# Whole turns of a cosine through an integer tile, and another queue order where layer 2 begins

## The chip, the cores and the metric

The kernel runs on one core of one Trainium2 chip. The metric is the device time of one execution in microseconds (us); lower is better. Before the change the median of three runs is 1700.83 us (1698.61 to 1701.08). Engines are named as in the profile: PE is TensorE's matmuls, PEld its weight loads, DVE is VectorE, ACT is ScalarE, POOL is GpSimd, and SP is the queue that issues the DMAs. All loads and stores of this kernel stand in that one queue.

## What is computed

Attention over 8 batches, 8 heads, 576 positions, with keys and values averaged in groups of 8; its output is 4608 tokens of 512 columns. Two layers follow, each of 512 by 2048 by 512:

```python
def _moe_ref(x, w_in, w_out):        # layer 1
    h = x @ w_in
    g = h * np.cos(h)
    return (g @ w_out).astype(np.float32)

def _moe2_ref(x, w_in, w_out):       # layer 2
    h = x @ w_in
    relu6 = np.clip(h + 3.0, 0.0, 6.0)
    g = h * relu6 / 6.0
    return (g @ w_out).astype(np.float32)
```

## The kernel before

Every number of the matmuls is split into a high part, written by ACT as fp32r, and a low part, the difference, made by DVE or POOL; a product is three matmuls: high by high, high by low, low by high.

**Layer 1** walks over 144 steps. A step is one block of 512 tokens by 128 columns of the hidden layer: `gemm1` makes `h` in PSUM with 12 matmuls, a chain turns `h` into `g` = h cos(h), and `gemm2` takes `g` two steps later with 12 more. The chain of a step is, in program order: ACT `t` = h/2π + 0.25 (L288); ACT `g` = t + MAGIC, which rounds t to whole turns (L293); DVE `g` = (g − MAGIC) − t (L294); ACT `g` = sin(−2π g) (L297); DVE `g` = h·g (L301); ACT `gh`, the high part (L304); DVE or POOL `gl`, the low part (L310). Attention is cut into pieces that are recorded between the steps by a table of due numbers (`GOFF`), so that attention and layer 1 share the engines until about 450 us. Later steps carry, in the same way, the conversion of layer 2's weights (`quads`), which leave for `s_d` in DRAM, and the first seven operands of layer 2 (`split_small`).

**Layer 2** works on pairs of token blocks, `PAIRS`: the first has 256 columns a block, the other four 512. For each pair it runs seven products for each of four groups g (Strassen's scheme, class `Quad`): product n of group g takes the weight tile `wt[0, g, n]` and the operand `ops[pb, n]`. Twelve matmuls make one product. Between them, `Quad.end` evacuates: L899 and L910 (ACT) copy banks after product 1, L912 (DVE) adds after product 2, L917 (DVE) after product 4, and the function `gate` runs for products 3 to 6: ACT L970 (relu into a tile of the ring `take_r`), DVE L971 (times the input), and a store to `g_d` (L974). Product 4 needs L912 done, since it goes on in the bank that L912 reads; product 6 needs L917 in the same way.

The operands of the next pair are made by `make_op` (body `operand`): for some n a sum of input quarters (L705, L707, L709, L714), then the high part on ACT (L711), then the low part (L712). Their inputs come by four loads from `y_d` (`load_raw`, L851). Weight tiles come by `load_w` (L839), 28 for a layer half.

The order on each engine is set by a scheduler that takes the recorded program and its own estimates of durations; each engine then executes in that order, and an instruction that waits holds up all behind it on its engine. `tc.issue_after(x)` records that what is issued inside the block on the engine of x stays behind x there; it adds no wait on another engine.

Of the kernel before, what the change touches and what calls it, by code (L numbers as in the profile page):

```python
# [8 lines left out]
F32 = mybir.dt.float32  # L9
F32R = mybir.dt.float32r  # L10
BF16 = mybir.dt.bfloat16
U32 = mybir.dt.uint32
AF = mybir.ActivationFunctionType
# [6 lines left out]
MAGIC = 12582912.0  # L20
# [9 lines left out]
def tile_kernel(ctx, tc, q, k, v, wi1, wo1, wi2, wo2, ident_d, mask_d, out):  # L30
# [119 lines left out]
    def fetch_quads(m, u):  # L150
        wi, wo = words[1]
        for half in range(2):
            st = stg.tile([P, 2 * HW], U32, tag="st", name="st", bufs=2)
            for part in range(2):
                o = part if half else 1 - part
                if m == 0:
                    g, c = divmod(u, 2)
                    col = (o * (NF // 2) + 2 * g) * P * 2
                    src = wi[(half * 2 + c) * P : (half * 2 + c + 1) * P, col : col + HW]
                else:  # L160
                    row = (half * (NF // 2) + u) * P
                    src = wo[row : row + P, o * HW : (o + 1) * HW]
                nc.sync.dma_start(out=st[:, part * HW : (part + 1) * HW], in_=src)
            staged["q", m, u, half] = st

    def quads(m, u):

        wa = stg.tile([P, 1024], U32, tag="a", name="wa", bufs=2)
        wb = stg.tile([P, 1024], F32, tag="wb", name="wb", bufs=1)
        halves = {}  # L170

        def bits(half):
            st = staged["q", m, u, half]
            a = wa[:, half * HW : (half + 1) * HW]
            e = halves[half] = stg.tile([P, HW], BF16, tag="e", name="e")
            nc.scalar.activation(out=e, in_=st.bitcast(BF16)[:, 3::4], func=AF.Square)
# [9 lines left out]
        def value(half):  # L186
            st = staged.pop(("q", m, u, half))
            a = wa[:, half * HW : (half + 1) * HW]
# [5 lines left out]
                out=f(a), in0=halves[half], scalar=2.0**-30, in1=f(a), op0=ALU.is_ge, op1=ALU.mult  # L194
            )

        a21, a11, a12, a22 = (f(wa)[:, n * 256 : (n + 1) * 256] for n in range(4))
        s1, s2, s3, s4 = (wb[:, n * 256 : (n + 1) * 256] for n in range(4))

        def sums(part):  # L200
# [7 lines left out]
        def split(part):  # L208
            n, k0 = ((3, 0), (4, 3))[part]
            w = f(wa)[:, 256:] if part == 0 else wb  # L210
            at = 4 * (u % 2) + 2 * part
            hi, lo = (big(CONV[at + x])[:, : n * 256] for x in range(2))
# [3 lines left out]
            for h, t in ((0, hi), (1, lo)):  # L216
                if m == 0:
                    g, c = divmod(u, 2)
                    dst = d[g * 7 + k0 : g * 7 + k0 + n, :, c, h, :]
                else:  # L220
                    q, c = divmod(u, 2)
                    dst = d[q + 4 * k0 : q + 4 * (k0 + n - 1) + 1 : 4, :, c, h, :]
                nc.sync.dma_start(
                    out=dst.rearrange("t p x -> p t x"),
                    in_=f(t).rearrange("p (t x) -> p t x", x=256),
                )

        def fetch():
            if (m, u) != (1, 7):
                fetch_quads(*divmod(8 * m + u + 1, 8))  # L230
# [4 lines left out]
            [lambda: bits(0)],  # L235
            [lambda: before(0)],
            [lambda: value(0)],
            [lambda: bits(1), lambda: before(1)],
            [lambda: value(1), fetch],
            [lambda: sums(0)],  # L240
            [lambda: sums(1)],
        ]

# [423 lines left out]
    def w_ahead(s, odd):  # L667
        nonlocal quad_at
        if not running:
            if converted == len(wjobs):  # L670
                if s < SA + LAG or s >= SB:
                    return
                if quad_at == 16 and not quad_ops:
# [7 lines left out]
                elif not quad_ops:  # L681
                    if quad_at == 0:
                        fetch_quads(0, 0)
                    quad_ops.extend(quads(*divmod(quad_at, 8)))
# [273 lines left out]
    for n in range(28):  # L958
        load_w(0, n)
    for pb, (t0, w) in enumerate(PAIRS):  # L960
# [111 lines left out]
```

## Time and profile before

| | |
|---|---|
| median of 3 runs | 1700.83 us |
| the profiled execution | 1703.01 us, of which the span is 1701.2 us |
| PE busy | 1622.8 us, 95% of the span |
| DVE, ACT, POOL busy | 1162.1, 952.1, 351.1 us |
| mean granted clock of TensorE | 0.987 of full speed |

The span has four stages: attention alone (to about 75 us), attention with layer 1 (to about 450 us), layer 1 with the conversion of layer 2's weights (to 996 us) and layer 2. The windows view gives, for a stretch, the busy time of each engine and the share of the clock that TensorE was granted; the timeline gives single instructions with the idle time of their engine before them; the lines view groups instructions by line. A PE that is busy in the view all the time has no hole there, and the number of its matmuls tells its pace.

### The profile page before, as it was taken

What the parts mean: (1) busy time and instruction counts of PE and PEld (TensorE: products, weight loads), DVE (VectorE), ACT (ScalarE), POOL (GpSimd) and SP (SyncE); (2) the same over time, 40 slices, a digit from 0 to 9 for tenths busy, and PEclk for the clock granted to TensorE, in tenths of its full rate; (3) what the DMA queues carried; (4) which work ended last, traced back from release to release, by engine and by line L of the source; (5) the groups of instructions that cost most, each with busy time, mean ns of one, the idle gap of its engine ahead of it and who ended that gap; (6) DMA issues with size and microseconds to landing.
All of it is one profiled execution on the core that took longest, in us unless ns stands there. A gap on an engine that the chain in (4) does not pass through costs nothing. (4 is left out here: it accounts for less than half of the span.)

```text
span 1701.2 us, 21102 instructions
## 1 busy us (share of the span) xinstructions
PE 1622.8 (95%) x7658; PEld 1349.7 (79%) x7658; DVE 1162.1 (68%) x1579; ACT 952.1 (56%) x1393; POOL 351.1 (21%) x266
## 2 busy tenths in 40 slices
PE   4588899999999999999999999999999999999999
PEld 3466677888888888888888788888888888888889
DVE  7899866665777788887886444454454576768665
ACT  2477778788666666665665533344444344444444
POOL 3656544232323201111113002020201000000000
PEclk9799999999999999999999998999999999999999
DMA  7555533322433377665665373242438955344231
GB/s 230 180 162 184 184 103 127 118 85 90 144 113 112 108 236 236 198 209 175 198 204 164 126 281 137 116 169 100 149 123 326 332 212 183 116 143 140 84 112 38
DMA packets 154758, 274.07 MB, mean 161 GB/s; under 512 B 15776, under 2 KB 79392, under 8 KB 153632
## 3 DMA queue, kind: packets, MB, share of 16 engines
q1 hardware_dynamic: 154656, 272.74, 48.1%
q8 instruction: 60, 0.98, 0.2%
q14 instruction: 42, 0.34, 0.1%
HBM read 167.84 MB, written 104.86 MB: 160 GB/s over the span
## 5 line engine op out<-in xcount | busy, mean ns | idle before, releaser
L859 PE MATMUL bank<-wa,wb 128*128 128x512 f32 (+1 forms) x1368 | 291.9, 361 | 6.7 <-issue 5.7
L859 PEld LDWEIGHTS bank<-wa,wb 128*128 128x128 f32 x1368 | 234.4, 192 | 45.2 <-issue 6.1
L281 PE MATMUL h<-xh,wb 128*128 128x512 f32 x648 | 211.4, 389 | 0.1
L324 PE MATMUL y<-gh,wb 128*128 128x512 f32 x648 | 210.8, 389 | 0.0
L711 ACT ACTIVATE wa<-wu 128x1024 fp32r<-128x1024 f32 (+1 forms) x130 | 127.3, 980 | 142.9 <-PE bank L859 124.9
L859 PE MATMUL bank<-wu,wb 128*128 128x512 f32 (+1 forms) x792 | 198.4, 386 | 0.0
L281 PE MATMUL h<-xh,wa 128*128 128x512 f32 x504 | 174.8, 405 | 2.8 <-DVE g L301 1.2
L294 DVE SCALAR_TENSOR_TENSOR g<-g,t 128x512 f32<-128x512 f32 x144 | 112.4, 781 | 95.0 <-ACT g L293 94.4
L859 PEld LDWEIGHTS bank<-wu,wb 128*128 128x128 f32 x792 | 148.7, 188 | 29.9
L324 PE MATMUL y<-gh,wa 128*128 128x512 f32 x504 | 171.1, 398 | 0.0
L259 POOL TENSOR_TENSOR xl<-xr,xh 128x512 fp32r<-128x512 f32 x72 | 105.5, 1481 | 315.2 <-ACT xh L258 308.2
L281 PEld LDWEIGHTS h<-xh,wb 128*128 128x128 f32 x648 | 121.6, 188 | 25.6 <-ACT xh L258 0.6
L324 PEld LDWEIGHTS y<-gh,wb 128*128 128x128 f32 x648 | 121.7, 188 | 25.3
L297 ACT ACTIVATE g<-g 128x512 f32<-128x512 f32 x144 | 90.9, 631 | 78.4 <-DVE g L294 77.9
L304 ACT ACTIVATE gh<-g 128x512 fp32r<-128x512 f32 x144 | 90.2, 627 | 71.0 <-DVE g L301 70.8
L712 DVE TENSOR_TENSOR wa<-wu,wa 128x1024 fp32r<-128x1024 f32 (+1 forms) x80 | 89.5, 1123 | 55.9 <-ACT wa L711 55.8
L281 PE MATMUL h<-xl,wb 128*128 128x512 f32 x324 | 126.3, 390 | 1.1 <-POOL xl L259 1.1
L324 PE MATMUL y<-gl,wb 128*128 128x512 f32 x324 | 126.0, 389 | 0.0
L301 DVE TENSOR_TENSOR g<-h,g 128x512 f32<-128x512 f32 x144 | 98.6, 685 | 30.9 <-ACT g L297 30.7
L859 PE MATMUL bank<-wa,wa 128*128 128x512 f32 (+1 forms) x552 | 117.5, 359 | 0.0
L970 ACT ACTIVATE wu<-bank,bias_c 128x1024 f32<-128x1024 f32 (+1 forms) x60 | 61.8, 1030 | 98.3 <-PE bank L859 85.3
L281 PEld LDWEIGHTS h<-xh,wa 128*128 128x128 f32 x504 | 95.3, 190 | 23.5 <-issue 2.0
(157 smaller groups left out, 3021.8 us busy)
## 6 DMA issues: line engine op xcount, KB each, us to landing
g_d<-wu SPq DMA_DIRECT2D x64, 512.0 KB
wu<-g_d SPq DMA_DIRECT2D x56, 512.0 KB
xr<-x_d SPq DMA_DIRECT2D x72, 256.0 KB
wb<-s_d SPq DMA_DIRECT2D x36, 512.0 KB
s_d<-wa SPq DMA_DIRECT2D x32, 512.0 KB
s_d<-wa SPq DMA_DIRECT2D x32, 384.0 KB
raw<-in_k_dram SPq DMA_DIRECT2D x8, 1152.0 KB
yp_d<-ys SPq DMA_DIRECT2D x36, 256.0 KB
```

Source lines behind the costliest of these rows:

```text
L259: nc.gpsimd.tensor_tensor(out=xl, in0=t, in1=f(xh), op=ALU.subtract)
L281: nc.tensor.matmul(h, a[:, cs], z, start=(n == 0), stop=(n == 3 * NC - 1))
L294: mark[s] = nc.vector.scalar_tensor_tensor(out=g, in0=g, scalar=MAGIC, in1=t, op0=ALU.subtract, op1=ALU.subtract)
L297: nc.scalar.activation(out=g, in_=g, func=AF.Sin, scale=-TWO_PI)
L301: nc.vector.tensor_tensor(out=g, in0=hs[s], in1=g, op=ALU.mult)
L304: nc.scalar.activation(out=gh, in_=g, func=AF.Copy)
L324: nc.tensor.matmul(y[c], a, z, start=(first and n == 0), stop=(last and n == 2))
L711: nc.scalar.activation(out=hi, in_=src, func=AF.Copy)
L712: el.tensor_tensor(out=lo, in0=src, in1=f(hi), op=ALU.subtract)
L859: nc.tensor.matmul(bank[:, e, :wide], w[:, j, h, e], z[:, j], start=start and j == 0 and x == 0, stop=stop and j == 1 and x == 2, skip_gro ...
L970: nc.scalar.activation(out=r, in_=c, func=AF.Relu, bias=bias_c[:, 2:3], scale=1.0)
```

## The change

In the chain, `t` becomes an int32 tile, so that the write of L288 rounds h/2π + 0.25 to a whole number of turns. The instruction with MAGIC (L293) goes. DVE's instruction now reads `h` from PSUM and the integer tile, h/2π − t, and the sine takes π/2 as a bias tile. In `quads` code is regrouped into a class; its instructions are the same in kind, size and number.

At the start of layer 2, 21 of 28 weight loads are recorded first, then the four input loads of pair 1; the other seven weight loads stand behind the last store of group 0. The operands of pair 1 are made during groups 2 and 3 (table `EARLY`) and no longer during group 1; ACT's and DVE's part of each operand is kept behind the last gate of that moment. Two sums of pair 1 go from POOL to DVE. The ring for the gate's results has five tiles and not three in groups 0 to 2 of the first pair. Input loads of later pairs stand behind the last store of group 0.

```diff
     def chain0(s):
         g = gpl.tile([P, N], F32, tag="g", name="g", bufs=2)
-        t = gpl.tile([P, N], F32, tag="t", name="t", bufs=2)
+        t = gpl.tile([P, N], I32, tag="t", name="t", bufs=2)
         nc.scalar.activation(out=t, in_=hs[s], func=AF.Copy, bias=0.25, scale=INV_2PI)
         gs[s] = (g, t)
 
     def chain1(s):
         g, t = gs[s]
-        nc.scalar.activation(out=g, in_=t, func=AF.Copy, bias=MAGIC, scale=1.0)
         mark[s] = nc.vector.scalar_tensor_tensor(
-            out=g, in0=g, scalar=MAGIC, in1=t, op0=ALU.subtract, op1=ALU.subtract
+            out=g, in0=hs[s], scalar=INV_2PI, in1=t, op0=ALU.mult, op1=ALU.subtract
         )
-        nc.scalar.activation(out=g, in_=g, func=AF.Sin, scale=-TWO_PI)
+        nc.scalar.activation(out=g, in_=g, func=AF.Sin, scale=TWO_PI, bias=bias_c[:, 1:2])
...
     take_r = turn_of(["u16", "u17", "u18"])
+    take_r0 = turn_of(["u16", "u17", "u18", "u12", "u13"])
...
         hi, lo = (cols(big(tag), w) for tag in XO[n])
-        operand(n, raws, hi, lo, {1: pool, 2: vec, 4: vec, 3: pool}.get(n), pool if n > 3 else vec)
+        sums = vec if pb == 1 else pool
+        with tc.issue_after(last["a"].ins), tc.issue_after(last["v"].ins):
+            operand(n, raws, hi, lo, {1: sums, 2: vec, 4: vec, 3: sums}.get(n), pool if n > 3 else vec)
         ops[pb, n] = hi, lo
...
-    for n in range(28):
+    last = {}
+    EARLY = {(2, 0): 0, (2, 3): 1, (2, 5): 2, (2, 6): 3, (3, 0): 4, (3, 4): 5, (3, 6): 6}
+    for n in range(21):
         load_w(0, n)
+    raws = load_raw(1)
...
-            if more and g == (pb > 0):
-                raws = load_raw(pb + 1)
+            if more and pb > 0 and g == 1:
+                with tc.issue_after(last["s"].ins):
+                    raws = load_raw(pb + 1)
 
             def gate(i, t, c, pb=pb, g=g, w=w):
-                r = cols(take_r(), w)
+                r = cols((take_r if pb or g == 3 else take_r0)(), w)
...
-                if more and (pb == 0) * 2 + g == 3:
-                    make_op(pb + 1, n, raws)
+                x = EARLY.get((g, n)) if pb == 0 else n if g == 3 else None
+                if more and x is not None:
+                    make_op(pb + 1, x, raws)
...
+            if pb == g == 0:
+                with tc.issue_after(last["s"].ins):
+                    for n in range(21, 28):
+                        load_w(0, n)
```

The scheduler sets a new order on each engine. Three places follow, each as it stood and as it stands. The lines of the changed program are up to some 25 higher: L970 is now L993, L711 is L727, L712 is L728, L912 is L928, L917 is L933, L971 is L996, L839 is L855, L851 is L867.

**ACT, where layer 2 begins.** Before, from the bank copies of group 1 on:

```order
L899 ACTIVATE bank<-bank 128x2x256
L910 ACTIVATE wu_9291<-bank 128x512
L711 ACTIVATE wu_9272<-wu_9142 128x1024
L711 ACTIVATE wu_9293<-wu_9146 128x1024
L711 ACTIVATE wu_9332<-wu_9148 128x1024
L970 ACTIVATE wu_9255<-bank,bias_c 128x512
L711 ACTIVATE wu_9311<-wu_9142 128x1024
L970 ACTIVATE wu_9328<-bank,bias_c 128x512
L970 ACTIVATE wu_9351<-wu_9349,bias_c 128x512
```

Now, from the bank copies of group 1 to those of group 2:

```order
L915 ACTIVATE bank<-bank 128x2x256
L926 ACTIVATE wu_9143<-bank 128x512
L993 ACTIVATE wu_9170<-bank,bias_c 128x512
L993 ACTIVATE wu_9188<-wu_9186,bias_c 128x512
L993 ACTIVATE wu_9204<-bank,bias_c 128x512
L993 ACTIVATE wu_9220<-bank,bias_c 128x512
L727 ACTIVATE wu_9237<-wu_8984 128x1024
L915 ACTIVATE bank<-bank 128x2x256
```

Three high parts of pair 1 stood ahead of a gate of group 0 (the tile 9255) and of all gates of group 1; now no high part stands ahead of a gate of these two groups.

**DVE, groups 2 and 3 of the first pair.** Before, group 2 and the first sum of group 3:

```order
L912 TENSOR_TENSOR bank<-bank,wu_9428 128x2x256
L971 SCALAR_TENSOR_TENSOR wu_9455<-wu_9455,bank 128x512
L917 TENSOR_TENSOR wu_9471<-bank,wu_9428 128x512
L971 SCALAR_TENSOR_TENSOR wu_9473<-wu_9473,wu_9471 128x512
L971 SCALAR_TENSOR_TENSOR wu_9489<-wu_9489,bank 128x512
L971 SCALAR_TENSOR_TENSOR wu_9505<-wu_9505,bank 128x512
L912 TENSOR_TENSOR bank<-bank,wu_9537 128x2x256
```

Now, from the first gate of group 2 to the first sum of group 3:

```order
L996 SCALAR_TENSOR_TENSOR wu_9283<-wu_9283,bank 128x512
L721 TENSOR_TENSOR wu_8988<-wu_8986,wu_8988 128x1024
L933 TENSOR_TENSOR wu_9304<-bank,wu_9256 128x512
L728 TENSOR_TENSOR wu_9288<-wu_8988,wu_9287 128x1024
L996 SCALAR_TENSOR_TENSOR wu_9306<-wu_9306,wu_9304 128x512
L996 SCALAR_TENSOR_TENSOR wu_9322<-wu_9322,bank 128x512
L723 TENSOR_TENSOR wu_8984<-wu_8988,wu_8984 128x1024
L996 SCALAR_TENSOR_TENSOR wu_9343<-wu_9343,bank 128x512
L728 TENSOR_TENSOR wu_9348<-wu_8990,wu_9347 128x1024
L728 TENSOR_TENSOR wu_9327<-wu_8984,wu_9326 128x1024
L730 TENSOR_TENSOR wu_8990<-wu_8990,wu_8984 128x1024
L928 TENSOR_TENSOR bank<-bank,wu_9385 128x2x256
```

Operand work that stood in group 1 now stands here: one sum (L721) ahead of group 2's L933, and three 1024-wide operations ahead of group 3's L928.

**PE, attention beside layer 1.** The stretch behind the scores (L452, now L468) of a unit of attention. Before:

```order
L504 MATMUL ap_ps<-ident,e_106 128x128 x4
L281 MATMUL h<-xh,wa_417 128x512
L281 MATMUL h<-xh,wa_416 128x512
L281 MATMUL h<-xl,wa_416 128x512
L281 MATMUL h<-xh,wa_417 128x512
L281 MATMUL h<-xh,wa_416 128x512
L526 MATMUL ap_ps<-ident,e_109 128x128
L526 MATMUL ap_ps<-ident,e_106 128x128
L281 MATMUL h<-xl,wa_416 128x512
L452 MATMUL ap_ps<-kbd_104,qT 128x144 x2
```

Now:

```order
L298 MATMUL h<-xh,wa_417 128x512
L298 MATMUL h<-xh,wa_416 128x512
L298 MATMUL h<-xl,wa_416 128x512
L298 MATMUL h<-xh,wa_417 128x512
L298 MATMUL h<-xh,wa_416 128x512
L520 MATMUL ap_ps<-ident,e_106 128x128 x4
L542 MATMUL ap_ps<-ident,e_109 128x128
L542 MATMUL ap_ps<-ident,e_106 128x128
L298 MATMUL h<-xl,wa_416 128x512
L298 MATMUL h<-xh,wa_417 128x512
L340 MATMUL y_848<-gh,wa_205 128x512
L340 MATMUL y_848<-gl,wa_205 128x512
```

The transposes of unit 106 moved behind five matmuls of layer 1, and the next unit's scores, which stood right behind, follow only after a step's twelve products of `gemm2` and two more matmuls.

## Rows read from the trace of the kernel before

**Rows 1.** The page: busy time by engine, and the chain that ended last.

```profile
PE 1622.8 (95%) x7658; PEld 1349.7 (79%) x7658; DVE 1162.1 (68%) x1579; ACT 952.1 (56%) x1393; POOL 351.1 (21%) x266
PE 39%; ACT 0%; issue 0%
```

**Rows 2.** Windows: stretch and length, busy time and instructions by engine, granted clock, DMA.

```profile
core 0: us, PE busy (x) PEld busy (x) DVE busy (x) ACT busy (x) POOL busy (x), PEclk, DMA share, GB/s
75.00:100.00 25.00, 19.97 (x100) 14.22 (x99) 23.64 (x40) 16.35 (x29) 17.00 (x13) 0.98 0.37 109
100.00:150.00 50.00, 41.82 (x207) 32.26 (x206) 48.41 (x76) 37.39 (x61) 32.19 (x25) 0.97 0.62 193
150.00:200.00 50.00, 41.67 (x202) 33.09 (x201) 46.12 (x66) 37.98 (x67) 31.26 (x26) 0.97 0.59 191
200.00:250.00 50.00, 46.87 (x233) 38.09 (x234) 32.24 (x60) 35.85 (x60) 21.77 (x21) 0.97 0.37 112
250.00:300.00 50.00, 47.18 (x249) 39.30 (x248) 34.45 (x61) 40.99 (x67) 23.56 (x22) 1.00 0.40 129
300.00:450.00 150.00, 149.11 (x764) 124.39 (x763) 96.11 (x179) 117.98 (x197) 41.34 (x36) 1.00 0.32 104
450.00:900.00 450.00, 450.00 (x1987) 372.63 (x1986) 359.83 (x546) 285.24 (x473) 81.87 (x55) 1.00 0.56 178
900.00:950.00 50.00, 48.73 (x213) 39.48 (x212) 31.54 (x43) 28.76 (x48) 18.89 (x13) 1.00 0.37 111
1000.00:1050.00 50.00, 43.34 (x316) 41.85 (x316) 24.22 (x29) 20.39 (x28) 14.89 (x6) 0.90 0.60 212
1021.40:1031.60 10.20, 7.64 (x35) 7.08 (x34) 6.11 (x7) 3.32 (x5) 3.07 (x2) 0.50 0.38 125
1050.00:1650.00 600.00, 600.00 (x2649) 496.81 (x2648) 357.15 (x303) 265.21 (x253) 34.37 (x14) 1.00 0.46 164
```

**Rows 3.** Timeline from 1006 us, layer 2's beginning: start, length, instruction, idle before.

```profile
1006.20 6.04 PE L859 MATMUL bank<-wa,wb 128*128 128x256 f32 x49
...
1013.66 2.41 POOL L705 TENSOR_TENSOR wu<-wu,wu 128x1024 f32<-128x1024 f32 x1 [72.82 <-DMA wu<-y_d]
1016.09 2.00 ACT L711 ACTIVATE wu<-wu 128x1024 fp32r<-128x1024 f32 x2 [3.98 <-POOL wu L705]
...
1018.00 0.67 ACT L970 ACTIVATE wu<-bank,bias_c 128x512 f32<-128x512 f32 x1
...
1020.11 3.08 DVE L712 TENSOR_TENSOR wu<-wu,wu 128x1024 fp32r<-128x1024 f32 x1
...
1020.29 1.99 PE L859 MATMUL bank<-wa,wb 128*128 128x256 f32 x12 [4.10 <-issue]
...
1023.89 2.90 PE L859 MATMUL bank<-wa,wb 128*128 128x256 f32 x12 [1.61 <-issue]
...
1027.73 12.04 PE L859 MATMUL bank<-wa,wb 128*128 128x256 f32 x84 [0.95 <-ACT bank L899]
```

**Rows 4.** Lines by form, 996 to 1050 us: count, busy us, mean ns, idle before.

```profile
L912 DVE TENSOR_TENSOR bank<-bank,wu 128x512 f32<-128x512 f32 x4 | 2.8, 700 | 14.2 <-PE bank L859 14.2
L971 DVE SCALAR_TENSOR_TENSOR wu<-wu,bank 128x512 f32<-128x512 f32 x11 | 7.5, 684 | 6.7 <-ACT wu L970 6.7
L970 ACT ACTIVATE wu<-wu,bias_c 128x512 f32<-128x512 f32 x4 | 2.9, 722 | 4.5 <-DVE wu L917 4.5
L709 DVE TENSOR_TENSOR wu<-wu,wu 128x1024 f32<-128x1024 f32 x1 | 1.2, 1212 | 0.0
```

**Rows 5.** Lines, 150 to 300 us: the chain's instructions beside attention.

```profile
L294 DVE SCALAR_TENSOR_TENSOR g<-g,t 128x512 f32<-128x512 f32 x17 | 16.4, 968 | 6.3 <-ACT g L293 6.2
L301 DVE TENSOR_TENSOR g<-h,g 128x512 f32<-128x512 f32 x18 | 12.3, 682 | 5.6 <-ACT g L297 5.4
L297 ACT ACTIVATE g<-g 128x512 f32<-128x512 f32 x18 | 11.4, 631 | 10.5 <-DVE g L294 10.4
L293 ACT ACTIVATE g<-t 128x512 f32<-128x512 f32 x17 | 10.7, 629 | 0.4
```

**Rows 6.** Lines, whole span: an operation of mixed types, and one on strided integers.

```profile
L193 DVE SCALAR_TENSOR_TENSOR wa<-e,wa 128x512 f32<-128x512 bf16 x32 | 23.0, 719 | 0.2
L131 DVE SCALAR_TENSOR_TENSOR a<-st,a 128x512 uint32<-128x512 uint32 x32 | 28.8, 901 | 0.7
```

More of the change, by code (lines that the diff above doesn't have):

```diff
@@ L147, in convert_weights @@
         return [first, second, third]
[L150 to L176, printed above, removed]
+    class Unit:
+        def __init__(self, m, u, x=256, o=0):
+            self.m, self.u, self.x, self.o = m, u, x, o
+        def fetch(self, tile):
+            m, u, x = self.m, self.u, self.x
+            wi, wo = words[1]
+            self.st = []
+            for half in range(2):
+                st = tile(half)
+                for part in range(2):
+                    o = part if half else 1 - part
+                    if m == 0:
+                        g, c = divmod(u, 2)
+                        row, col = (half * 2 + c) * P, (o * (NF // 2) + 2 * g) * P * 2
+                    else:
+                        row, col = (half * (NF // 2) + u) * P, o * HW
+                    col += 2 * self.o
+                    src = (wi, wo)[m][row : row + P, col : col + 2 * x]
+                    nc.sync.dma_start(out=st[:, 2 * part * x : 2 * (part + 1) * x], in_=src)
+                self.st.append(st)
+        def begin(self, wa, wb, e):
+            self.wa, self.wb, self.e = wa, wb, e
+        def bits(self, half):
+            st, n = self.st[half], 2 * self.x
+            a = self.wa[:, half * n : (half + 1) * n]
+            self.flag = self.e()[:, :n]
+            nc.scalar.activation(out=self.flag, in_=st.bitcast(BF16)[:, 3::4], func=AF.Square)
@@ L184, in bits, with value @@
             )
-        def value(half):
-            st = staged.pop(("q", m, u, half))
-            a = wa[:, half * HW : (half + 1) * HW]
+        def value(self, half):
+            st, n = self.st[half], 2 * self.x
+            a = self.wa[:, half * n : (half + 1) * n]
             nc.vector.scalar_tensor_tensor(
@@ L193, in value, with sums @@
             nc.vector.scalar_tensor_tensor(
-                out=f(a), in0=halves[half], scalar=2.0**-30, in1=f(a), op0=ALU.is_ge, op1=ALU.mult
+                out=f(a), in0=self.flag, scalar=2.0**-30, in1=f(a), op0=ALU.is_ge, op1=ALU.mult
             )
-        a21, a11, a12, a22 = (f(wa)[:, n * 256 : (n + 1) * 256] for n in range(4))
-        s1, s2, s3, s4 = (wb[:, n * 256 : (n + 1) * 256] for n in range(4))
-        def sums(part):
+        def sums(self, part):
+            x = self.x
+            a21, a11, a12, a22 = (f(self.wa)[:, n * x : (n + 1) * x] for n in range(4))
+            s1, s2, s3, s4 = (self.wb[:, n * x : (n + 1) * x] for n in range(4))
             if part == 0:
@@ L206, in sums, with split @@
                 nc.vector.tensor_tensor(out=s4, in0=a12, in1=s2, op=ALU.subtract)
-        def split(part):
+        def split(self, part, tile):
+            x, m = self.x, self.m
             n, k0 = ((3, 0), (4, 3))[part]
-            w = f(wa)[:, 256:] if part == 0 else wb
-            at = 4 * (u % 2) + 2 * part
-            hi, lo = (big(CONV[at + x])[:, : n * 256] for x in range(2))
+            w = f(self.wa)[:, x : 4 * x] if part == 0 else self.wb
+            hi, lo = (tile(part, h, n * x) for h in range(2))
             nc.scalar.activation(out=hi, in_=w, func=AF.Copy)
@@ L234, in quads, with fetch_quads @@
         return [
-            [lambda: bits(0)],
+            [lambda: unit.bits(0)],
             [lambda: before(0)],
[L237 to L241, printed above, removed]
-        ]
+            [lambda: unit.value(0)],
+            [lambda: unit.bits(1), lambda: before(1)],
+            [lambda: unit.value(1), fetch],
+            [lambda: unit.sums(0)],
+            [lambda: unit.sums(1)],
+        ]
+    def fetch_quads(n):
+        units[n].fetch(lambda half: stg.tile([P, 2 * HW], U32, tag="st", name="st", bufs=2))
     unsplit = []
@@ L672, in w_ahead @@
                     return
-                if quad_at == 16 and not quad_ops:
+                if quad_at == len(units) and not quad_ops:
                     if unsplit:
```

40 lines of the change are left out of this document (23 added, 17 removed).

## Prediction

> **What bounds the kernel now.** I read the page first: PE is busy for 95% of the span, and the chain that ended last is PE alone [rows 1]. So the question is only where PE has holes, and the windows answer it [rows 2]. From 450 to 900 us PE is busy all the time, 1987 matmuls in 450 us, 226.5 ns each, and from 1050 to 1650 us the same, 2649 in 600 us, again 226.5 ns. Nothing that the change does to ACT, DVE or a queue can shorten these stretches; it can only open holes in them. Three places have holes. (1) From 75 to 450 us PE idles 5.0 + 8.2 + 8.3 + 3.1 + 2.8 + 0.9 = 28.3 us. There DVE is the fullest engine at first (23.64 of 25, 48.41 and 46.12 of 50 us up to 200 us), then ACT (35.85 and 40.99 of 50 us up to 300 us). (2) From 900 to 950 us PE idles 1.3 us. (3) From 1000 to 1050 us, where layer 2 begins, it idles 6.7 us and the granted clock is 0.90.
>
> The timeline of that last place shows the cause [rows 3]. PE stops after the products of group 1 for 4.10 us, then for 1.61 and 0.95 us. ACT's gate instruction L970 at 1018.00 us, whose bank PE needs again, stood behind two high parts (L711) of pair 1's operands, which had waited 3.98 us for POOL's sum L705, which had waited for its load from `y_d`. The work that PE needed at once was queued behind work for 20 us later. The clock then stood at 0.50, the 1.2 GHz level, for 10.2 us [rows 2], behind the idle 4.10 us.
>
> **The change, part by part. Layer 2's beginning.** The hole costs 6.7 us of idle time, plus the slow clock: in 1021.4 to 1031.6 us PE did 35 matmuls in 7.64 us busy; at the pace ahead of the hole, 49 in 6.04 us or 0.123 us each [rows 3], they take 4.3 us. That is 3.3 us more, 10.0 in all. The new order on ACT has no high part ahead of a gate in groups 0 and 1, so that this wait can't arise there. The input loads of pair 1 now stand ahead of seven weight loads. Those seven are needed one by one from group 3 on, 31 us after layer 2 begins (three groups of 84 matmuls at 0.123 us), the last at about 40 us, and stand behind stores that leave after some 12 us; seven tiles of 0.52 MB are 3.7 MB, and at the 212 GB/s of that stretch [rows 2] they take 17 us. The last arrives some 11 us early, so I cost them at nothing; their cover is groups 1 and 2, and a rate under 130 GB/s would use it up. The two more ring tiles take away waits of the gate for its stores and cost nothing.
>
> What is late next is DVE, which has the operands to make in groups 2 and 3. In group 2 the sum L721 stands ahead of L933. After product 3 come the gate's ACT part (0.67 us [rows 3]), its DVE part (0.68), the sum (1.21) and L933 (0.70): 3.3 us with rows of the same widths [rows 4]. Products 4 and 5 last 2 x 12 x 0.123 = 2.9 us, so that product 6 waits about 0.4 us, or 0.6 with some 0.05 us at each hand-over. In group 3 three 1024-wide operations, 3.6 us, stand between the last gate of group 2 and L928, whose result product 4 needs. From the end of group 2's products, the last gate needs 0.7 + 0.7 us, behind a backlog of about 2 us from group 2; 2 + 1.4 + 3.6 + 0.7 = 7.7 us, against four products, 5.9 us, that PE has to do: 1.8 us of waiting. Together 2.4 us. Bounds: none, if the backlog is smaller, and 6.1 us, if both POOL and DVE stretch each other: DVE's L712 at 1020.11 us took 3.08 us in place of 1.2 beside POOL's work [rows 3], and two such stretches are 3.7 us. I take 2.4, since DVE's long operations ahead of L928 have no POOL work beside them in the new order. POOL's three low parts follow in group 3 and later. **Net: 10.0 - 2.4 = 7.6 us less.**
>
> **The chain.** Per step ACT loses L293, 0.629 us [rows 5]. The sine gets a bias tile: the sine before took 631 ns, a relu with a bias tile on the same width from SBUF 722 [rows 4], so that it may cost 0 to 0.09 us more; I take 0.09. ACT's write of integers isn't shown by any row; I take L288's time as it is. On DVE, L294 reads two SBUF tiles and took 968 ns on average from 150 to 300 us, while L301, which reads `h` from PSUM and one SBUF tile, took 682 [rows 5]. The new instruction has L301's operands, so I take 682; a mix of types (bf16 and fp32) takes 719, and the upper end is 901, an operation on strided integers [rows 6].
>
> From 450 us on all this lies beside a full PE and is worth nothing. From 150 to 300 us DVE saves 17 x 0.286 = 4.9 us, which I count in full since DVE sets the pace for a third of it and attention hands its delay on. ACT saves 17 x 0.54 = 9.2 us in the same stretch, but PE idles only 5.9 us in 200 to 300 us, where ACT is the fuller one, at 77%; a load that falls by 6.5 us in 76.8, some 8%, takes about 0.5 us of that. Against it stands the new order on PE: the next unit's scores follow 15 matmuls of layer 1 later at one place. PE is not the full engine there, but DVE, which is, may wait for its scores; at 226.5 ns the eight matmuls by which, counted in the two orders, attention's pieces of some three units lie later on average cost 1.8 us once. Further on the two orders keep step. Net 4.9 + 0.5 - 1.8 = 3.6 us less. Bounds: 10.8 less (4.9 and all 5.9 us of ACT's stretch), and 5 more, if the displaced pieces cost at three places and DVE gains nothing.
>
> On that contention the Trainium skill (SBUF — State Buffer, section Who interferes with whom) says that a VectorE instruction with two SBUF inputs shares a read port with GpSimd, and one of the two blocks until the other is done, while one with a single SBUF input doesn't. By that rule L294's longer times would go entirely, as in the sum, and POOL, which makes most low parts there, would gain too; by the rows alone POOL's gain isn't priced.
>
> **900 to 950 us.** PE idles 1.3 us there. A shorter chain on ACT may free it; I take half, 0.6 us, between 0 and 1.3.
>
> **Sum.** The span of 1701.2 us, with 1.8 us around it, is the profiled 1703.0 us; 7.6 + 3.6 + 0.6 = 11.8 us less give 1691.2 there. The profiled execution lies 2.2 us above the median of the runs, so 1700.8 - 11.8 = **1689.0 us** is the forecast.
>
> **The rivals.** (A) DVE becomes the bound at layer 2's beginning. The waits in groups 2 and 3 grow to 6.1 us by the stretch above, and the clock falls to 0.50 again for the 3.3 us: 9.4 of the 10.0 us are gone, and only 0.6 + 3.6 + 0.6 = 4.8 us remain, 1696 us. For it: L712 at 3.08 us. Against it: PE idled 1.3 us around 940 us and the clock stayed at 1.00 [rows 2].
>
> The same rule of the skill speaks for (A), since the two sums that go from POOL to DVE have two SBUF inputs each.
>
> (B) The chain is worth much more. In the attention stretch ACT is in the way of DVE oftener than its share tells: DVE idled 6.3 us before L294, 6.2 of them for L293, which is gone [rows 5]. With the full 10.8 us there, the time is 1700.8 - 7.6 - 10.8 - 0.6 = 1681.8 us. Against it: up to 200 us DVE hardly idles. (C) The integers don't do what they are for: ACT's write or DVE's read of them is slower, 901 ns on DVE. Then DVE gains 17 x 0.067 = 1.1 us, less than the 1.8 of the order: 1700.8 - 7.6 + 0.7 - 0.6 = 1693.3 us. (D) Slower than before: the new order on PE starves DVE beside attention. Each time that scores stand 15 matmuls later, 3.4 us, and DVE has nothing else, attention slips by that much. To eat up the 8.2 us of the other two places and end 3.4 us above before takes 11.6 us, four such places without any gain on DVE; six places, with DVE's 4.9 us kept, give 1700.8 - 8.2 - 4.9 + 20.4 = 1708.1 us. For it: DVE is nearly full up to 200 us. Against it: one such place is seen, and after it the two orders run level.
>
> **How the numbers follow.** The forecast has 0.58, with its own range 1684 to 1694 us. (A) has 0.12, (B) 0.17, (C) 0.06, (D) 0.07. The range for 8 in 10 takes in the forecast's and (C)'s, most of (B) and half of (A): 1681 to 1697 us. A measurement of this kernel tells 0.2%, 3.4 us, from no change. Faster than 1697.4 us are the forecast, (B), (C) and less than half of (A): 0.86. Within 0.2% is the rest of (A): 0.07. Slower is (D): 0.07.
>
> **What would show it.** In the profile after, the stretch 1000 to 1050 us should show PE idle for 1 to 4 us and the clock at 1.00. DVE's instruction on `h` and `t` should take about 0.68 us throughout, never over 1 us; the sine 0.63 to 0.72 us. The full stretches must keep their 226.5 ns per matmul. Layer 2 should begin some 4 us sooner than at 996 us. The prediction is wrong if PE's idle time in 75 to 450 us grows, if group 3 waits for weights, or if new holes open in the stretches that were full.

## The result, and the profile after

The changed kernel takes 1680.61 us (median of 4 runs, 1678.92 to 1681.6) against 1699.72 us for the kernel before, timed beside it: a ratio of 0.9888, with a 95% interval of [0.9871, 0.9905]. The gain is 19.1 us; 11.8 were forecast, and 1680.6 lies just below the range that began at 1681. The profiled execution took 1681.6 us, with a span of 1679.8.

The page of the kernel after: busy time by engine, the granted clock by slice, and the chain that ended last.

```profile
PE 1615.1 (96%) x7658; PEld 1345.9 (80%) x7658; DVE 1140.6 (68%) x1581; ACT 883.7 (53%) x1249; POOL 331.0 (20%) x264
PEclk7799999999999999999999999999999999999999
PE 87%; DVE 5%; DMA 3%; ACT 2%; POOL 2%; issue 1%; SPq 0%; ACTq 0%; POOLq 0%; DVEq 0%
```

ACT is busy for 68 us less than in [rows 1], DVE for 21.5, and neither number is the gain. Windows of the kernel after, with the columns of [rows 2]:

```profile
75.00:100.00 25.00, 21.23 (x111) 15.56 (x110) 23.64 (x42) 16.60 (x27) 15.19 (x15) 1.00 0.42 124
100.00:150.00 50.00, 44.86 (x236) 35.56 (x235) 49.53 (x84) 41.10 (x69) 32.49 (x27) 1.00 0.67 209
150.00:200.00 50.00, 44.14 (x216) 36.06 (x215) 37.47 (x60) 34.82 (x60) 28.05 (x24) 0.93 0.56 181
250.00:300.00 50.00, 48.18 (x252) 40.21 (x251) 34.43 (x64) 37.52 (x58) 17.25 (x19) 1.00 0.34 109
450.00:900.00 450.00, 450.00 (x1987) 372.63 (x1986) 349.16 (x549) 243.76 (x387) 73.19 (x52) 1.00 0.58 181
900.00:950.00 50.00, 50.00 (x223) 41.39 (x222) 29.09 (x40) 23.61 (x38) 17.90 (x12) 1.00 0.33 104
1000.00:1050.00 50.00, 50.00 (x314) 45.14 (x314) 28.92 (x31) 24.67 (x31) 7.59 (x3) 1.00 0.44 166
```

Against [rows 2]: PE executes 111, 236 and 216 matmuls up to 200 us where it executed 100, 207 and 202. The full stretch still has 1987 in 450 us. From 900 to 950 us there are 223 in place of 213. From 1000 to 1050 us PE no longer idles, and the clock stays at 1.00.

Three marks in the two traces (the start of the last attention matmul, of layer 2's first matmul, and of its last) split the whole difference of the two spans, 21.4 us (the profile before lies above its median, so that this is 2.3 us more than the gain by the medians):

| stage, us | before | after | difference |
|---|---|---|---|
| to the last attention matmul | 425.1 | 414.9 | −10.2 |
| from there to layer 2 | 570.8 | 568.6 | −2.2 |
| layer 2 | 701.3 | 692.3 | −9.0 |
| behind its last matmul | 4.0 | 4.0 | 0 |

Half of the difference thus lies in attention, where 3.6 us were expected. The chain's instructions have the durations that were expected. Lines of the kernel after, 150 to 300 us (count, busy us, mean ns, idle before):

```profile
L313 ACT ACTIVATE g<-g,bias_c 128x512 f32<-128x512 f32 x18 | 13.0, 722 | 5.3 <-DVE g L310 5.1
L310 DVE SCALAR_TENSOR_TENSOR g<-h,t 128x512 f32<-128x512 f32 x18 | 12.3, 685 | 4.4 <-ACT t L305 4.4
L305 ACT ACTIVATE t<-h 128x512 int32<-128x512 f32 x18 | 10.7, 592 | 16.9 <-PE h L298 16.9
```

DVE's instruction fell from 968 ns (L294 in [rows 5]) to 685, the sine rose from 631 to 722, and the write of integers takes 592, as the float write L288 did in this stretch before. POOL's low part of the chain, which the sum had not priced, fell from 1485 to 1342 ns in this stretch; the last section tells what that goes with.

### The profile page after: what moved, and what is told of

Its sections match the earlier page's. It is cut to its first block, busy times and chain, and to the rows that moved or that the text cites. A ratio compares the mean times of both kernels' runs of the same rounds, so it can differ in the third digit from the quotient of the medians.

```text
span 1679.8 us, 21085 instructions
## 1 busy us (share of the span) xinstructions
PE 1615.1 (96%) x7658; PEld 1345.9 (80%) x7658; DVE 1140.6 (68%) x1581; ACT 883.7 (53%) x1249; POOL 331.0 (20%) x264
## 4 chain that ended last, share of the span: by engine, by line
PE 87%; DVE 5%; DMA 3%; ACT 2%; POOL 2%; issue 1%; SPq 0%; ACTq 0%; POOLq 0%; DVEq 0%
PE bank L875 41%; PE h L298 21%; PE y L340 21%; PE ap_ps L555 2%; PE ap_ps L468 1%; DMA raw<-in_v_dram 1%; DMA raw<-in_k_dram 1%; DMA xr<-x_d 1%; DVE raw L423 1%; DVE sm L490 1%; PE ap_ps L520 1%; POOL xl L276 1%; DVE ptl L525 0%; POOL e L494 0%; DVE e L479 0%
## 5 line engine op out<-in xcount | busy, mean ns | idle before, releaser
L875 PE MATMUL bank<-wa,wb 128*128 128x512 f32 (+1 forms) x1368 | 287.7, 358 | 0.0
L727 ACT ACTIVATE wa<-wu 128x1024 fp32r<-128x1024 f32 (+1 forms) x130 | 127.3, 980 | 142.6 <-PE bank L875 121.2
L310 DVE SCALAR_TENSOR_TENSOR g<-h,t 128x512 f32<-128x512 f32 x144 | 99.0, 688 | 104.6 <-ACT t L305 104.3
L276 POOL TENSOR_TENSOR xl<-xr,xh 128x512 fp32r<-128x512 f32 x72 | 100.0, 1401 | 324.6 <-ACT xh L275 319.5
L305 ACT ACTIVATE t<-h 128x512 int32<-128x512 f32 x144 | 85.5, 593 | 126.0 <-PE h L298 125.7
L313 ACT ACTIVATE g<-g,bias_c 128x512 f32<-128x512 f32 x144 | 104.2, 724 | 79.4 <-DVE g L310 78.9
L728 DVE TENSOR_TENSOR wa<-wu,wa 128x1024 fp32r<-128x1024 f32 (+1 forms) x80 | 89.5, 1123 | 56.9 <-ACT wa L727 56.8
```

Of the source, the lines that this page charges most:

```text
L276: nc.gpsimd.tensor_tensor(out=xl, in0=t, in1=f(xh), op=ALU.subtract)
L305: nc.scalar.activation(out=t, in_=hs[s], func=AF.Copy, bias=0.25, scale=INV_2PI)
L310: mark[s] = nc.vector.scalar_tensor_tensor(out=g, in0=hs[s], scalar=INV_2PI, in1=t, op0=ALU.mult, op1=ALU.subtract)
L313: nc.scalar.activation(out=g, in_=g, func=AF.Sin, scale=TWO_PI, bias=bias_c[:, 1:2])
L727: nc.scalar.activation(out=hi, in_=src, func=AF.Copy)
L728: el.tensor_tensor(out=lo, in0=src, in1=f(hi), op=ALU.subtract)
```

## The experiments

### The two halves apart

x1_cos is the kernel before with the chain's diff alone; x2_l2 is the changed kernel with the old chain.

> The kernel before with the cosine's change alone; layer 2 as before. If the two parts are independent, layer 1 ends as in the changed kernel, 12.4 us sooner than before (983.4 us and not 995.8 us on the profile), and the hole where layer 2 begins stays: about 1688 us. If the queue order of layer 2 had a share in the sooner end of layer 1, it ends later than 983 us.

> The changed kernel with the cosine as before (L293 and two SBUF operands on DVE). If the parts are independent, layer 1 ends at 996 us as before and only the hole of 9 us where layer 2 begins is gone: about 1691 us. The first PE wait of over 1 us behind 960 us should be missing.

Measured: x1_cos 1686.93 us, ratio 0.9929 [0.9915, 0.9944]; x2_l2 1691.37 us, ratio 0.9952 [0.9937, 0.9967]; the kernel before 1698.71 us there. The chain earns 11.8 us alone, layer 2's order 7.3, together 19.1. Each ratio's interval is some 5 us wide, so that the exact sum is luck; but the halves add up within that, layer 2's half is near the 7.6 us forecast for it, and the miss lies in the chain. In x1_cos attention ends at 412.2 us and layer 2's hole is still there; in x2_l2 attention ends at 422.7 us, and the hole is gone.

### The chain: which of its two savings

x3_sbuf lets DVE read two SBUF tiles again; x4_act gives ACT its extra step back. x3_sbuf changes what the cosine computes.

```
# x3_sbuf
-            out=g, in0=hs[s], scalar=INV_2PI, in1=t, op0=ALU.mult, op1=ALU.subtract
+            out=g, in0=t, scalar=INV_2PI, in1=t, op0=ALU.mult, op1=ALU.subtract
# x4_act
+        nc.scalar.activation(out=t, in_=t, func=AF.Copy, scale=1.0)
```

> The changed kernel, but DVE's instruction of the chain reads the integer tile twice and not h from PSUM: two SBUF operands as before, and still no extra ACT instruction (the argument of the cosine is wrong by that). Theory: DVE's time, stretched where two-SBUF instructions meet POOL, sets attention's pace; then attention ends late again, near 423 us (before 425, changed 415), and the time is about 1688 us. Rival, the ACT instruction that went is what counts: attention ends at 415 us and the time is 1681 us.

> The changed kernel with one more ACT instruction in the chain, a copy of the integer tile in place (0.6 us, the load and the length of the chain as before); DVE reads h from PSUM. Theory: attention ends near 416 us and the time is about 1682 us, since DVE's time is as in the changed kernel. Rival, ACT's load or the chain's length counts: attention ends near 425 us and the time is about 1690 us.

Measured: x3_sbuf 1687.17 us, ratio 0.9926 [0.9911, 0.9941]; x4_act 1683.9 us, ratio 0.9909 [0.9892, 0.9925]. From x2_l2's 1691.4 us, ACT's saving alone is then worth 4.2 us and DVE's alone 7.5. That reads like "DVE sets the pace", so the next pair took DVE's load away by another way: the addition of 1e-9 to the softmax sums, 40 instructions, is left out of the changed kernel (x5_no_eps) and of x2_l2 (x11_old_no_eps).

```
-        nc.vector.tensor_scalar(out=sm[:w], in0=sm[:w], scalar1=1e-9, scalar2=None, op0=ALU.add)
```

> The changed kernel without DVE's addition of 1e-9 to the sums of the softmax (L491, one instruction of 8 columns a unit, 40 in all; a sum of at least 1 in fp32 is left as it was by that addition). Theory, DVE's time is attention's time: the 12 of these instructions that lie between the attention matmuls 180 and 420 took 5.5 us there; that stretch shrinks by about 5 us, and by some 2 more before it, so that the time is about 1674 us. Rival, PE's order or ACT sets the pace there: within 2 us of the changed kernel's 1680.6.

> As the run before this one, but with the cosine as before (the old chain, the new order of layer 2, no addition of 1e-9). In that order the 12 additions took 9.5 us of DVE, 789 ns each, in the same stretch. Theory: attention's stretch shrinks by 7 to 9 us against the kernel with the new order of layer 2 alone, to about 1683 us in all. Rival: it stays at 1691 us.

Measured: x5_no_eps 1678.63 us, 0.9887 [0.9872, 0.9902]; x11_old_no_eps 1689.45 us, 0.9948 [0.9931, 0.9964]. From the 181st attention matmul to the last, DVE is busy for 12 and 14 us less than in the kernels that they come from. The medians are 2 us lower in both, the ratios by 0.0001 and 0.0004, well within their intervals. That DVE's busy time is passed on one to one, which would have brought 1674 and 1683 us, is refuted. But all four kernels have a weakness: the scheduler gave each an order of its own on every engine (in x3_sbuf some 200 of DVE's 1581 places differ from the changed kernel's), so that none shows an instruction's worth alone.

### Instructions and order apart

Kernels of this kind have two things that differ, the instructions and the order in which each engine issues them. The order can be held fixed. At the end of the program, each instruction is tied to the one that is to stand ahead of it on its engine, with an edge that sets the order and adds no wait:

```
+    for engine, deltas in orders.items():        # places as the other kernel has them
+        at, prev, mine = 0, None, real[engine]
...
+        for step in deltas:
+            at += step
+            if prev is not None:
+                tc.add_manual_dep(
+                    mine[at], prev.name,
+                    mybir.DependencyInfo(mybir.DependencyClass.NoSync, mybir.DependencyReason.DATA),
+                    reason="order",
+                )
+            prev = mine[at]
```

> The kernel with layer 2's change and the old cosine chain (1691.4 us; attention ends at 422.7 us), but every engine issues its instructions in the order that the changed kernel has; the 144 roundings on ScalarE stand one place behind the write of t. If the shorter instructions earn the chain's 10 us, nothing changes: 1691 us, attention's end at about 423 us. If the scheduler's new order earns them, the time falls to that of the changed kernel, 1681 us, attention's end at about 413 us, with DVE's instruction of the chain still near 900 ns and ScalarE as busy as before. Between the two, the share tells.

> The changed kernel, all its instructions as they are, but every engine issues them in the order of the kernel with layer 2's change and the old chain. If the instructions earn the 10 us: 1681 us, attention's end at about 413 us. If the new order earns them: 1691 us and 423 us, although DVE's instruction of the chain takes 680 ns and ScalarE has 144 instructions less. If both are needed, both pinned kernels stay near 1691 us; if either is enough, both come to 1681 us.

Measured: x12_old_chain_new_order 1707.27 us, ratio 1.0042 [1.0027, 1.0056], so slower than the kernel before; x13_new_chain_old_order 1684.17 us, 0.9907 [0.9887, 0.9927]. Neither expectation had it that the new order harms the old chain. Part of that is where the step stands that the new order has no place for, ACT's rounding: in x12_old_chain_new_order another ACT instruction comes between the write of `t` and the rounding in 56 of 144 steps. The four corners (old or new chain, old or new order) were then timed side by side, in x15_old_chain_new_order with the rounding always directly behind the write of `t`.

> The changed kernel once more, beside the three others: 1680.6 us by the first result; attention's end within 3 us of 414.9 us. New instructions, new order.

> The kernel with layer 2's change and the old chain once more: 1691.4 us by the first look. Old instructions, old order.

> New instructions, old order, once more. If the instructions alone earn all, it equals r_after (1680.6 us). By the first run they earn 7 of the 10.8 us: 1684 us. If the first run was a lucky one and the order is what counts, it comes near r_old_chain (1691 us).

> Old instructions, new order, with the rounding on ScalarE always directly behind the write of t. If the 1707 us of the run before came from where the rounding stood, this comes down to about 1688 us, order alone then being worth some 3 us. If the new order doesn't fit the old chain, it stays above 1700 us, with holes behind 450 us as before.

| median, us (ratio, 95% interval) | old order | new order |
|---|---|---|
| old chain | 1688.91 (0.9943 [0.9927, 0.996]) | 1695.82 (0.9978 [0.9968, 0.9987]) |
| new chain | 1685.54 (0.9918 [0.9902, 0.9935]) | 1678.86 (0.9876 [0.9854, 0.9897]) |

The instructions alone earn 3.4 us in the old order. The new order alone costs 6.9 us. Both together earn 10.1. In the new order the instructions are thus worth 17.0 us, five times as much as in the old one; by the intervals, about 13 to 21 us against 0 to 8. x15_old_chain_new_order came out between its two expectations: moving the rounding took back 11.5 of x12_old_chain_new_order's 1707.27 us, and the rest of the loss stayed. So the 17.0 us hold for this place of the rounding, and would be more for the other. The windows show more (columns as in [rows 2]). First r_after, new chain in the new order:

```profile
75.00:175.00 100.00, 86.29 (x442) 66.88 (x442) 95.69 (x162) 75.51 (x126) 64.46 (x57) 0.99 0.58 178
175.00:425.00 250.00, 245.40 (x1255) 203.88 (x1254) 161.22 (x303) 183.05 (x293) 87.28 (x83) 0.99 0.38 122
```

r_old_chain, old chain in the old order:

```profile
75.00:175.00 100.00, 82.45 (x392) 63.68 (x391) 95.41 (x146) 70.59 (x121) 60.51 (x49) 0.93 0.57 178
175.00:425.00 250.00, 242.09 (x1254) 199.85 (x1254) 168.70 (x307) 201.37 (x331) 100.32 (x89) 1.00 0.36 115
```

r_new_chain_old_order:

```profile
75.00:175.00 100.00, 84.55 (x409) 65.41 (x408) 95.33 (x151) 69.48 (x116) 57.58 (x49) 0.94 0.57 178
175.00:425.00 250.00, 243.90 (x1259) 200.87 (x1258) 162.23 (x309) 187.30 (x300) 94.62 (x90) 1.00 0.37 119
```

x15_old_chain_new_order:

```profile
75.00:175.00 100.00, 85.19 (x438) 65.51 (x436) 96.30 (x162) 79.56 (x134) 62.72 (x53) 1.00 0.57 176
175.00:425.00 250.00, 236.78 (x1212) 195.89 (x1213) 158.59 (x294) 193.78 (x318) 91.76 (x85) 0.99 0.36 115
```

In the first 100 us the order decides: 442 and 438 matmuls in the new one, 392 and 409 in the old one, nearly whatever the chain (all other profiles of the new order have 438 to 443, and those of the old one 397 to 407). The granted clock is 0.99 and 1.00 against 0.93 and 0.94; it is not the order's alone, since x16_sbuf_new_order below, in the new order too, has 0.96 there with 439 matmuls. In the next 250 us the new order needs the new chain: 1255 matmuls with it, 1212 without, while the old order does 1254 and 1259 with either. There the old chain in the new order gives back 42 of the 46 matmuls that it was ahead (of the old chain's two profiled executions, x15_old_chain_new_order's lies 2.7 us below its kernel's median and r_old_chain's 3.4 us above; they are 0.8 us apart where the medians are 6.9, so that the loss itself is shown by the times and not by these windows). The first profile of the changed kernel has 1243 matmuls there, so that 12 of the 43 between 1255 and 1212 can be scatter.

Two last kernels keep the new order and give back one of the two savings each: the changed kernel with DVE's two SBUF reads (x16_sbuf_new_order), and with ACT's extra step (x17_act_new_order). The edits are those of x3_sbuf and x4_act.

> The changed kernel, every engine in the changed kernel's order, but DVE's instruction of the chain reads the integer tile twice (two SBUF operands in place of h from PSUM and one of SBUF; this changes what the cosine computes). If the reads are what the new order can't bear: DVE's instruction near 0.9 us and 1690 us or more. If ScalarE's extra step is: 1679 to 1683 us, although DVE's instruction is as long.

> The changed kernel in the changed kernel's order, with one more ScalarE instruction per step that rewrites t in place, directly behind the write of t. If ScalarE's extra step is what the new order can't bear: 1690 us or more, with a stall near 940 us. If the reads are: 1679 to 1683 us. If the two add up, the two losses make 17 us together.

Measured: x16_sbuf_new_order 1683.93 us, 0.9906 [0.9891, 0.9922]; x17_act_new_order 1688.33 us, 0.9932 [0.992, 0.9945]; the kernel before 1699.25 us there. Against r_after's ratio of 0.9876, the reads cost 5.1 us and ACT's step 9.5, which makes 14.6 of the 17 us. r_after was timed on another occasion, and the intervals leave about 1 to 10 us for the reads and 5 to 14 for the step; between the two kernels, timed together, it is 4.4 us, 1 to 8. So both matter, and ACT's step more. That step is a whole one of 632 ns, where the change saves ACT 0.54 us a step net of the slower sine. The waits of PE, 175 to 425 us (line that waits, line waited for: us in total, times, longest), name the place (scores are L468 in r_after, L469 and L470 in the two others). r_after:

```profile
PE ap_ps L468 <- DVE ptl L525: 3.2, 3, 1.9
```

The changed kernel's first profile (after):

```profile
PE ap_ps L468 <- DVE ptl L525: 5.2, 4, 2.1
```

x17_act_new_order:

```profile
PE ap_ps L469 <- DVE ptl L526: 7.3, 7, 3.0
```

x15_old_chain_new_order:

```profile
PE ap_ps L470 <- DVE ptl L527: 9.6, 7, 3.8
```

PE's scores wait for a bank that DVE frees with `ptl`. What holds DVE up is seen in its lines, 150 to 300 us, in x17_act_new_order:

```profile
L311 DVE SCALAR_TENSOR_TENSOR g<-h,t 128x512 f32<-128x512 f32 x18 | 12.4, 690 | 11.0 <-ACT t L310 10.9
```

The instruction takes as long as in the changed kernel, 690 against 685 ns. But DVE stands idle ahead of it for 11.0 us in place of 4.4, waiting for ACT's `t`, with all of attention's work queued behind. In x15_old_chain_new_order that is 11.4 us; in the old order it is 4.9 us with the old chain and 3.3 with the new one. This fits a longer chain that passes through ACT and holds up DVE, whose instructions stand in one order in both kernels. That it is the chain's length and not ACT's load is argued from these waits and not shown: no run gives ACT the same step outside the chain.

DVE's reads tell another story in the new order. x16_sbuf_new_order, 150 to 300 us:

```profile
L310 DVE SCALAR_TENSOR_TENSOR g<-t 128x512 f32<-128x512 int32 x17 | 12.6, 740 | 4.5 <-ACT t L305 2.8 <-POOL e L494 1.3 <-POOL e L496 0.3
```

With two SBUF reads the instruction takes 740 ns here and 757 in x15_old_chain_new_order, where it took 968 before and 948 in r_old_chain. So how far two SBUF reads stretch it depends on the order too.

What the new order gains with either chain, the traces locate. From the 44th to the 76th of attention's transposing matmuls PE does the same work but for two matmuls. r_new_chain_old_order, then r_after:

```profile
93.34:170.57 77.23, 64.70 (x310) 50.69 (x310) 73.98 (x114) 55.11 (x91) 44.10 (x38) 0.93 0.60 188
92.40:161.20 68.80, 59.88 (x312) 47.46 (x311) 68.16 (x111) 54.85 (x91) 42.03 (x37) 1.00 0.64 199
```

The new order is 8.4 us shorter there. PE's idle time falls by 3.6 us of that, and its busy time by 4.8, with the granted clock at 1.00 in place of 0.93. This is also where the two orders differ most on PE: from the 40th to the 75th transposing matmul 3 to 15 more matmuls of layer 1 stand ahead in the new order (at two of the 36 none), and behind that the orders are never more than 5 apart. With the old chain the stretch takes 77.8 us in r_old_chain and 70.5 in x15_old_chain_new_order. From the 76th to the 121st the new order is the longer one, 99.4 us against 96.2 with the new chain and 104.1 against 99.9 with the old. Which moved instruction does it, on PE or on another engine, was not isolated. Nor is it shown that a scheduler's order fits its own instructions best, or worst: x3_sbuf in its own order took 1687.17 us and x16_sbuf_new_order with the same instructions 1683.93, x4_act 1683.9 and x17_act_new_order 1688.33, and the intervals of either pair overlap.

### Layer 2's beginning

x7_free lets the operands' parts go free of the last gate; x6_group1 makes pair 1's operands in group 1 again, with the fence and with three ring tiles; x8_loads records all 28 weight loads ahead of pair 1's input loads.

```
# x7_free (and x7_free_again)
-        with tc.issue_after(last["a"].ins), tc.issue_after(last["v"].ins):
-            operand(n, raws, hi, lo, ...)
+        operand(n, raws, hi, lo, ...)
# x6_group1
-    EARLY = {(2, 0): 0, (2, 3): 1, (2, 5): 2, (2, 6): 3, (3, 0): 4, (3, 4): 5, (3, 6): 6}
+    EARLY = {(1, n): n for n in range(7)}
-                r = cols((take_r if pb or g == 3 else take_r0)(), w)
+                r = cols(take_r(), w)
# x8_loads
-    for n in range(21):
+    for n in range(28):
         load_w(0, n)
-            if pb == g == 0:
-                with tc.issue_after(last["s"].ins):
-                    for n in range(21, 28):
-                        load_w(0, n)
```

> The changed kernel with the operands of pair 1 (and later pairs) recorded at the same moments but not kept behind the last gate on ACT and DVE: the scheduler then puts high parts of pair 1 back among the gates of groups 0 and 1. If that fence is what closes the hole, PE idles again for several us in the first 45 us of layer 2, some 1686 to 1690 us; if the earlier input loads are enough, no hole of over 1 us and 1681 us.

> The changed kernel with the operands of pair 1 made during group 1, as before, and not in groups 2 and 3, still behind the last gate; the gate's ring has three tiles, since two of the five are needed for operands. If the later moment is needed, DVE and ACT fall behind in group 1 and PE idles 2 us or more there; if the fence and the earlier loads are enough, under 1 us.

> The changed kernel without the fence that keeps an operand's parts behind the last gate, timed this time. One look gave 1675.5 us, 5 us under the changed kernel, with 0.5 us of that in layer 2 and the rest in attention, where its instructions and their order are the same. If that rest is scatter from run to run, the median is 1680 us; if the kernel is faster, 1676 us.

> The changed kernel with all 28 weight loads ahead of pair 1's input loads again. If late inputs made the hole, and moving the operands to groups 2 and 3 is enough to hide them, layer 2's beginning stays within 1 us of the changed kernel (about 0.6 us lost up to 1025 us). If the loads' order is what closes it, 3 to 8 us come back, as a wait of the first operands in group 2 with a gate behind them.

These are read from layer 2 itself, from its first matmul to its 1681st, since attention scatters by some us. The kernel before takes 355.8 us for that, the changed kernel 346.8, x6_group1 348.8, x8_loads 347.4, x7_free 345.0 in both of its profiles. None of the three has the hole (x6_group1 took 1680.46 us and x8_loads 1678.52, one run each). Late inputs with late operands and the fence cost 0.6 us (x8_loads), operands in group 1 with early inputs and the fence 2 us (x6_group1). The hole is seen only where late inputs, early operands and no fence come together, as x1_cos has them (356.1 us). Each of the three runs puts back one of the three and none brings the hole back; whether one change alone would close it, no run shows.

x7_free alone has no wait at all in layer 2. What the fence costs is seen around 1253 us in the changed kernel; timeline (start, length, instruction, idle before):

```profile
1253.13 2.67 POOL L728 TENSOR_TENSOR wa<-wu,wa 128x1024 fp32r<-128x1024 f32 x1 [1.81 <-PE bank L875]
...
1253.46 3.42 DVE L725 TENSOR_TENSOR wu<-wu,wu 128x1024 f32<-128x1024 f32 x1
...
1256.92 1.06 ACT L727 ACTIVATE wu<-wu 128x1024 fp32r<-128x1024 f32 x1 [2.41 <-DVE wu L725]
1257.88 1.04 ACT L727 ACTIVATE wa<-wu 128x1024 fp32r<-128x1024 f32 x1
...
1258.83 1.00 ACT L915 ACTIVATE bank<-bank 128x1024 f32<-128x1024 f32 x1
...
1259.89 6.46 PE L875 MATMUL bank<-wu,wa 128*128 128x512 f32 x27 [1.10 <-ACT bank L915]
```

DVE's sum with two SBUF reads starts 0.33 us behind POOL's low part and takes 3.42 us where such sums take 1.22 alone; ACT waits 2.41 us for it, the bank's copy L915 stands behind, and PE loses 1.5 us against its pace. Timed, x7_free_again took 1677.77 us, 0.9864 [0.9842, 0.9886], and x7_free, one run, 1675.47. By the intervals it can't be told from r_after (0.9876 [0.9854, 0.9897]); the 1.8 us of layer 2 are seen in its profiles alone.

## Why the prediction was wrong, and where it was right

**Layer 2's beginning was right: −7.6 forecast, −9.0 measured.** The hole's size was right: 10.0 us in the sum, 10.8 by the traces (355.8 less the 345.0 of x7_free_again). The new waits were put at 2.4 us, and they are 1.8 (346.8 less 345.0), most of them at another place, so that the size agrees in part by luck. Where they were expected they hardly appear. Timeline of the kernel after:

```profile
1008.82 11.08 PE L875 MATMUL bank<-wa,wb 128*128 128x256 f32 x89
...
1011.00 1.22 DVE L721 TENSOR_TENSOR wu<-wu,wu 128x1024 f32<-128x1024 f32 x1
...
1012.13 0.68 DVE L933 TENSOR_TENSOR wu<-bank,wu 128x512 f32<-128x512 f32 x1
...
1019.74 2.23 PE L875 MATMUL bank<-wu,wa 128*128 128x512 f32 x9
...
1020.91 0.69 DVE L928 TENSOR_TENSOR bank<-bank,wu 128x512 f32<-128x512 f32 x1
...
1021.81 4.47 PE L875 MATMUL bank<-wa,wu 128*128 128x256 f32 x36
```

L721 does stand ahead of L933, yet PE runs on. In group 3 L928 does stand behind 1024-wide operations, but nine 512-wide matmuls of the next pair, 2.23 us, are queued on PE at 1019.74, and they cover most of the wait for L928, which ends at 1021.60. The step counted DVE's queue and not PE's. Rival (A)'s mechanism, DVE stretched beside POOL, came once, at 1253 us, for 1.5 us. The rule of the Trainium skill (SBUF — State Buffer, section Who interferes with whom) that two SBUF inputs on VectorE and a GpSimd read exclude each other agrees with those 3.42 us, which end 1.08 us behind POOL's instruction, and with L310, which has one such input and kept to 685 ns.

**900 to 950 us: −0.6 forecast, −2.2 measured.** The stall is gone as a whole, ten matmuls of 226.5 ns each. In x16_sbuf_new_order and x17_act_new_order PE still waits 0.9 and 0.7 us there for POOL's `xl`, so either saving left out brings a part of it back.

**The chain was the step that failed: −3.6 forecast, −10.2 measured.** The term that failed is the order's. It had the wrong sign: +1.8 us was put for scores that stand later on PE, and with the new chain the new order earns 6.7 (r_new_chain_old_order against r_after). The sum charged the displaced pieces as a delay of attention and put nothing for what they do to PE's waits, which fall by 3.6 us in the stretch where they stand, with the clock higher by 0.07.

The terms for the instructions, 4.9 of DVE and 0.5 of ACT, were worked out from rows of the old order, and there the two savings together earn 3.4 us: less than the sum has, but within the noise. What failed is that they were taken to hold in any order. In the new one the same two savings are worth 17.0 us, ACT's step 9.5 by x17_act_new_order where 0.5 stood, and DVE's reads 5.1 by x16_sbuf_new_order. That these 5.1 meet the 4.9 forecast is luck: 4.9 was counted from 968 ns, and in x16_sbuf_new_order the instruction takes 740, which makes 0.9 us in 17 steps. ACT's term came from shares: a load that falls by 8% takes 8% of PE's idle time. But the step stands in a row of dependent work, where it can be a wait of DVE's; [rows 5] showed 6.2 us of idle time ahead of L294 for L293, and the sum left them to rival (B).

**The rivals.** (B), 1681.8 us, was the nearest by its number, and by its mechanism in part: ACT's step does hold DVE up in the new order. But (B) gave the whole gain to the instructions, and in the old order they don't have it. Its reason against, that DVE hardly idles up to 200 us, fails as the order changes what that stretch holds: from 150 to 200 us DVE is busy for 37.47 us in place of 46.12. (C) fell with 685 ns. (D), that the new order starves DVE, has its like in the old chain (+6.9 us, with PE's wait for `ptl` at 9.6 us); with the new chain it doesn't happen.

## What to carry to other kernels

Where a scheduler sets the order, an edit comes as two, its instructions and a new order, which can be worth as much and of either sign; pin the order before an experiment is read as the worth of an instruction. For a step taken out of a dependent chain, look at the wait of the engine behind it, and not only at the share of its own engine: the share gave 0.5 us here, and the new order 9.5. And before a wait is charged, look at what the waiting engine has queued ahead of it: other work there may cover the wait.

## What was not expected of the hardware

Seven profiles have the changed kernel's layer 1, instructions and order alike (the changed kernel twice, x1_cos, x6_group1, x7_free twice, x8_loads). Their attention ends between 410.6 and 414.9 us, the first profile's 414.9 being the latest, so that effects of some 3 us in that stage need several executions. Three profiles with the old chain and order have 422.7 to 425.1.

Where an order adds waits in that stage, TensorE's clock falls too, and the two together cost more than the waits: 8.4 us against 3.6 between the two windows above, with the clock at 0.93 and 1.00. In r_new_chain_old_order one stretch at 0.50, from 111.5 to 118.3 us, begins inside a wait of PE of 2.93 us.

POOL's low parts of the chain became shorter more with the order than with DVE's reads. From 150 to 300 us they take 1499 ns in r_old_chain and 1429 and 1484 in the two profiles of the new chain in the old order; in the new order 1329 in x15_old_chain_new_order and 1361 in x16_sbuf_new_order, with two SBUF reads, and 1342 in the changed kernel, with one.
